# Layer scale on one core: pieces of 53, 11, 53, 11 rows with five loads, in place of 40, 37, 40, 11 with seven

## The chip, the cores and the metric

One of the eight cores of a Trainium2 chip. The metric is the device time of one execution in microseconds (us).

## The reference

```python
B, S, D = 1024, 16, 512          # bfloat16: x, y of [B, S, D], gamma of [D]
def reference(x, y, gamma):
    return x + gamma * y
```

That is 16,384 rows of 512 elements: 16.78 MB of x, as much of y, and as much to write.

## The kernel before

Each of the 128 partitions holds 128 rows of 1 KB. y has a buffer of its full size and the result is computed in it; x has one that is smaller than x, so a later load of x reuses the place of an earlier one. An entry of the list is one transfer: kind, first row, end row, and for x the place in its buffer.

```python
PIECES = [40, 37, 40, 11]       # VectorE's pieces
SP  = [('x', 0, 40, 0), ('y', 0, 40), ('x', 40, 77, 40), ('y', 40, 77),
       ('y', 77, 128), ('x', 77, 117, 0), ('x', 117, 128, 40)]      # queue of loads
ACT = [('g',), ('s', 0, 64), ('s', 64, 128)]                        # gamma, two stores
RELEASE = ('x', 77, 117, 0)     # its landing lets the first store go
DVE = [('m', 0), ('a', 0), ('m', 1), ('a', 1), ('m', 2), ('a', 2), ('m', 3), ('a', 3)]
# ... (cut)
            if need > known:                      # x: the adds that free its place
                eng.wait_ge(s_add, need)          # s: the adds that make its rows
# ... (cut)
        if kind == "m":                           # y = y * gamma
            need(y_loads, c)                      # wait for the loads of this piece
            nc.vector.tensor_tensor(out=yt, in0=yt, in1=g, op=MULT).then_inc(s_dve, 1)
            open_mults += 1
        else:                                     # y = x + y
            need(x_loads, c)
            if open_mults:                        # wait for the open multiplies
                _take(s_dve, open_mults, nc.vector)
                open_mults = 0
            at = x_at(starts[c])
            xt = x_sb[:, at : at + PIECES[c], :]
            nc.vector.tensor_tensor(out=yt, in0=xt, in1=yt, op=ADD).then_inc(s_add, 1)
```

gamma is spread over the partitions by a matmul with a row of ones and copied to SBUF. The first store waits for its adds and for the landing of the RELEASE load, so that it does not meet the loads in the DMA engines.

Of the kernel before, what the change touches and what calls it, by code (L numbers as in the profile page):

```python
# [3 lines left out]


PIECES = [40, 37, 40, 11]



SP = [('x', 0, 40, 0), ('y', 0, 40), ('x', 40, 77, 40), ('y', 40, 77), ('y', 77, 128), ('x', 77, 117, 0), ('x', 117, 128, 40)]  # L10
ACT = [('g',), ('s', 0, 64), ('s', 64, 128)]

EARLY = (2, 1)


RELEASE = ('x', 77, 117, 0)

DVE = [('m', 0), ('a', 0), ('m', 1), ('a', 1), ('m', 2), ('a', 2), ('m', 3), ('a', 3)]
MULT, ADD = mybir.AluOpType.mult, mybir.AluOpType.add


def _take(sem, n, eng):


    return eng.wait_ge(sem, n).then_inc(sem, -n)  # L25


def kernel(
# [18 lines left out]
    rows = N // P  # L47
    n = len(PIECES)
    assert sum(PIECES) == rows
    starts = [sum(PIECES[:c]) for c in range(n + 1)]  # L50
    dt = xf.dtype
# [7 lines left out]
    y_sb = nc.alloc_sbuf_tensor("y_sb", [P, rows, D], dt).ap()  # L59
    x_loads = [w for w in SP + ACT if w[0] == "x"]  # L60
    y_loads = [w for w in SP + ACT if w[0] == "y"]
    stores = [w for w in SP + ACT if w[0] == "s"]
    for loads in (x_loads, y_loads, stores):
# [8 lines left out]
    s_add, s_go, s_rel, s_end, s_out = sem("s_add"), sem("s_go"), sem("s_rel"), sem("s_end"), sem("s_out")  # L72
    added = [a for kind, *a in DVE if kind == "a"]
    order = {a[0]: k for k, a in enumerate(added)}

    def meets(a, b, c, d):
        return a < d and c < b

    def pieces_of(a, b):
        return [c for c in range(n) if meets(starts[c], starts[c + 1], a, b)]  # L80

    def x_at(row):
        return next(w[3] + row - w[1] for w in x_loads if w[1] <= row < w[2])

    def frees(w):

        old = x_loads[: x_loads.index(w)]
        old = [v for v in old if meets(v[3], v[3] + v[2] - v[1], w[3], w[3] + w[2] - w[1])]
        return [c for v in old for c in pieces_of(v[1], v[2])]

    early = []

    def ring(eng, what, n_early):

        known, went = 0, False
        for k, w in enumerate(what):
            kind = w[0]
            need = frees(w) if kind == "x" else pieces_of(w[1], w[2]) + list(w[3:]) if kind == "s" else []
            need = max((order[c] + 1 for c in need), default=0)
            if kind == "s" and not went:  # L100
                _take(s_go, 1, eng)
                went = True
            if need > known:
                eng.wait_ge(s_add, need)
                known = need
            if kind == "g":
                i = eng.dma_start(out=gamma_row, in_=gamma.unsqueeze(0)).then_inc(s_gamma, 16)
            elif kind == "x":
                to = x_sb[:, w[3] : w[3] + w[2] - w[1], :]
                i = eng.dma_start(out=to, in_=xv[:, w[1] : w[2], :]).then_inc(s_load[w], 16)  # L110
            elif kind == "y":
                r = slice(w[1], w[2])
                i = eng.dma_start(out=y_sb[:, r, :], in_=yv[:, r, :]).then_inc(s_load[w], 16)
            else:
                r = slice(w[1], w[2])
                i = eng.dma_start(out=ov[:, r, :], in_=y_sb[:, r, :]).then_inc(s_out, 16)
            if k < n_early:
                early.append(i.ins)

    ring(nc.sync, SP, EARLY[0])  # L120
    ring(nc.scalar, ACT, EARLY[1])
# [9 lines left out]

    _take(s_load[RELEASE], 16, nc.tensor)
    nc.tensor.sem_inc(s_go, 1)
# [4 lines left out]
    def need(loads, c):  # L138
        for w in loads:
            if w not in landed and meets(starts[c], starts[c + 1], w[1], w[2]):  # L140
                if w == RELEASE:
                    _take(s_rel, 1, nc.vector)
                else:
                    _take(s_load[w], 16, nc.vector)
                landed.add(w)

    for kind, *args in DVE:
        c = args[0]
        yt = y_sb[:, starts[c] : starts[c + 1], :]
        if kind == "m":  # L150
            need(y_loads, c)
            g = gamma_sb[:, None, :].to_broadcast([P, PIECES[c], D])
            nc.vector.tensor_tensor(out=yt, in0=yt, in1=g, op=MULT).then_inc(s_dve, 1)  # L153
            open_mults += 1
        else:
# [4 lines left out]
# [3 lines that stand above are left out]
# [44 lines left out]
```

## Time and profile before

| | before |
|---|---|
| time, median of 3 | 119.99 us (119.98 to 120.29) |
| span of the profiled run | 118.8 us |
| VectorE busy | 70.2 us, 59% |
| packets of both queues, share of 16 DMA engines | 98.6% |

The page gives busy time by engine and the share that the queues' packets take of all 16 DMA engines. The view by stretches gives, for each stretch of time, its length, the busy time of PE, PEld, DVE (VectorE) and POOL with the number of instructions, the granted clock, the mean DMA share and GB/s. A packet counts where it starts, so a short stretch can show a share over 1, and zero between two rounds of long packets that all engines are in. A hole is seen only when the next round's start comes later than the packet's length. The lines are in the prediction below.

### The profile page before, as it was taken

Reading aid. Unit: us, or ns where it says so; the run is one execution under the profiler, and the core shown is the slowest. Engines: PE = TensorE matmul, PEld = TensorE weight load, DVE = VectorE, ACT = ScalarE, POOL = GpSimd, SP = SyncE. Lnnn points to the kernel's source line nnn. Section 1 sums busy time; section 2 is a strip of 40 time slices with the busy share of each in tenths; the row PEclk is TensorE's granted clock in tenths of the full one; section 3 lists DMA queues with packets and bytes.
Section 4 is the critical chain, followed back from the end, with each engine's and each line's share of the span. In section 5 each row is a group of like instructions: output and inputs, shape, how many; then the busy total and the mean of one; then the engine's idle time right before and its main releaser. Section 6 shows DMA issues by size and latency. Waiting matters only on the chain. (4 is left out here: it accounts for less than half of the span.)

```text
span 118.8 us, 84 instructions
## 1 busy us (share of the span) xinstructions
PE 0.6 (0%) x1; PEld 0.1 (0%) x1; DVE 70.2 (59%) x10; POOL 0.2 (0%) x4
## 2 busy tenths in 40 slices
PE   0100000000000000000000000000000000000000
PEld 0000000000000000000000000000000000000000
DVE  0020000009999999799999999999999980000000
POOL 0000000000000000000000000000000000000000
DMA  7999999999999999989696999998899889988890
GB/s 221 442 441 441 441 441 441 441 425 408 408 421 472 485 459 408 475 369 563 281 563 262 441 414 441 408 637 353 353 530 530 353 353 397 662 353 353 353 684 22
DMA packets 1298, 50.33 MB, mean 424 GB/s; under 512 B 145, under 2 KB 146, under 8 KB 146
## 3 DMA queue, kind: packets, MB, share of 16 engines
q1 hardware_dynamic: 1008, 33.55, 66.0%
q10 hardware_dynamic: 290, 16.78, 32.6%
HBM read 33.56 MB, written 16.78 MB: 424 GB/s over the span
## 5 line engine op out<-in xcount | busy, mean ns | idle before, releaser
L153 DVE TENSOR_TENSOR y_sb<-y_sb,gamma_sb 128x20480 bf16<-128x20480 bf16 (+2 forms) x4 | 34.8, 8688 | 20.6 <-DVEq L25 20.6
L162 DVE TENSOR_TENSOR y_sb<-x_sb,y_sb 128x20480 bf16<-128x20480 bf16 (+2 forms) x4 | 34.8, 8691 | 0.6
L129 DVE CAST gamma_sb<-gamma_ps 128x512 bf16<-128x512 f32 x1 | 0.7, 690 | 4.1 <-DVEq L25 4.1
L124 DVE MEMSET ones_row<- 1x128 bf16 x1 | 0.2, 165 | 2.0 <-PEq L41 2.0
L127 PE MATMUL gamma_ps<-gamma_row,ones_row 1*128 1x512 bf16 x1 | 0.6, 581 | 5.5 <-PEq L25 5.5
L127 PEld LDWEIGHTS gamma_ps<-gamma_row,ones_row 1*128 1x128 bf16 x1 | 0.1, 98 | 5.5 <-issue 5.5
L191 POOL MEMSET const-bfloat16-1.0<- 128x1 bf16 x1 | 0.1, 102 | 0.0
L191 POOL MEMSET const-uint8-127<- 128x1 uint8 x1 | 0.1, 101 | 0.0
L191 POOL MEMSET const-float32-0.0<- 128x1 f32 x1 | 0.1, 99 | 0.2 <-issue 0.2
L191 POOL MEMSET const-float32-1.0<- 128x1 f32 x1 | 0.1, 98 | 0.0
## 6 DMA issues: line engine op xcount, KB each, us to landing
x_sb<-in_x_dram SPq DMA_DIRECT2D x2, 5120.0 KB, 21.3
y_sb<-in_y_dram SPq DMA_DIRECT2D x1, 6528.0 KB, 61.8
y_sb<-in_y_dram SPq DMA_DIRECT2D x1, 5120.0 KB, 26.3
x_sb<-in_x_dram SPq DMA_DIRECT2D x1, 4736.0 KB, 36.0
y_sb<-in_y_dram SPq DMA_DIRECT2D x1, 4736.0 KB, 46.9
x_sb<-in_x_dram SPq DMA_DIRECT2D x1, 1408.0 KB, 10.6
out_dram<-y_sb ACTq DMA_DIRECT2D x2, 21.8
gamma_row<-in_gamma_dram ACTq DMA_DIRECT2D x1, 1.0 KB
```

The source lines that it names most:

```text
L124: nc.vector.memset(ones_row, 1.0).then_inc(s_ones, 1)
L127: nc.tensor.matmul(gamma_ps, ones_row, gamma_row, start=True, stop=True).then_inc(s_ps, 1)
L129: nc.vector.tensor_copy(out=gamma_sb, in_=gamma_ps).then_inc(s_dve, 1)
L153: nc.vector.tensor_tensor(out=yt, in0=yt, in1=g, op=MULT).then_inc(s_dve, 1)
L162: nc.vector.tensor_tensor(out=yt, in0=xt, in1=yt, op=ADD).then_inc(s_add, 1)
L191: nc = _bacc.Bacc("TRN2", target_bir_lowering=False, num_devices=1)
```

## The change

Its intent is fewer, larger loads (five of 64, 64, 64, 53 and 11 KB a partition) that line up with the two 64-row stores, while the release of the first store stays with the last load but one.

```diff
-PIECES = [40, 37, 40, 11]
-SP = [('x', 0, 40, 0), ('y', 0, 40), ('x', 40, 77, 40), ('y', 40, 77), ('y', 77, 128), ('x', 77, 117, 0), ('x', 117, 128, 40)]
+PIECES = [53, 11, 53, 11]
+SP = [('y', 0, 64), ('x', 0, 64, 0), ('y', 64, 128), ('x', 64, 117, 0), ('x', 117, 128, 64)]
-RELEASE = ('x', 77, 117, 0)
+RELEASE = ('x', 64, 117, 0)
-DVE = [('m', 0), ('a', 0), ('m', 1), ('a', 1), ('m', 2), ('a', 2), ('m', 3), ('a', 3)]
+DVE = [('m', 0), ('m', 1), ('a', 0), ('a', 1), ('m', 2), ('m', 3), ('a', 2), ('a', 3)]
 # ... (cut: a load of x now waits only for the pieces whose rows it really
 #      overwrites, so the 53-row load waits for the first add alone)
```

I call the loads y0, x0, y1, x2, x3 in their order, and the adds first to last.

More of the change, by code (lines that the diff above doesn't have):

```diff
@@ L85, in frees @@
     def frees(w):
-        old = x_loads[: x_loads.index(w)]
-        old = [v for v in old if meets(v[3], v[3] + v[2] - v[1], w[3], w[3] + w[2] - w[1])]
-        return [c for v in old for c in pieces_of(v[1], v[2])]
+        c = set()
+        for v in x_loads[: x_loads.index(w)]:
+            lo, hi = max(v[3], w[3]), min(v[3] + v[2] - v[1], w[3] + w[2] - w[1])
+            if lo < hi:
+                c |= set(pieces_of(v[1] + lo - v[3], v[1] + hi - v[3]))
+        return sorted(c)
     early = []
```

## The prediction

> **What bounds the kernel now.** I read the page first: who is busy, and how many bytes move.
>
> ```profile
> span 118.8 us, 84 instructions
> ...
> PE 0.6 (0%) x1; PEld 0.1 (0%) x1; DVE 70.2 (59%) x10; POOL 0.2 (0%) x4
> ...
> q1 hardware_dynamic: 1008, 33.55, 66.0%
> q10 hardware_dynamic: 290, 16.78, 32.6%
> HBM read 33.56 MB, written 16.78 MB: 424 GB/s over the span
> ```
>
> VectorE works 59% of the span, but the packets of the two queues take 66.0 + 32.6 = 98.6% of what 16 DMA engines have. Every byte is needed once: x and y in, the result out. The chain of waits is no help here: it stops after one 3.09 us add, because what ends the span is a store that the chain does not count as work. So I cut the span into stretches and ask for the DMA share in each (last two columns: DMA share and GB/s). A packet is booked in the stretch where it starts, so I put the cuts in the pauses between rounds of packets.
>
> ```profile
> 0.00:1.00 1.00, 0.00 (x0) 0.00 (x0) 0.00 (x0) 0.20 (x4) 1.00 0.00 0
> 1.00:2.90 1.90, 0.00 (x0) 0.00 (x0) 0.17 (x1) 0.00 (x0) 1.00 1.15 345
> 2.90:48.00 45.10, 0.58 (x1) 0.10 (x1) 21.70 (x3) 0.00 (x0) 1.00 1.00 433
> 48.00:63.40 15.40, 0.00 (x0) 0.00 (x0) 14.59 (x3) 0.00 (x0) 1.00 1.01 434
> 63.40:75.60 12.20, 0.00 (x0) 0.00 (x0) 12.20 (x2) 0.00 (x0) 1.00 0.99 430
> 75.60:79.00 3.40, 0.00 (x0) 0.00 (x0) 3.40 (x1) 0.00 (x0) 1.00 0.93 394
> 79.00:98.30 19.30, 0.00 (x0) 0.00 (x0) 18.14 (x4) 0.00 (x0) 1.00 1.02 440
> 98.30:117.60 19.30, 0.00 (x0) 0.00 (x0) 0.00 (x0) 0.00 (x0) 1.00 1.00 435
> ```
>
> From 1.0 us to the end no stretch is idle. The 0.93 before 79.0 is made up by the 1.02 after it (two 11 KB packets' worth on the far side of the cut). Loads in pieces of 37 to 51 KB a partition and stores of 64 KB run at the same 433 GB/s. Above all there is no hole at 98.4, where the first store hands over to the second, nor at 79, where loads hand over to stores. The whole: 50.33 MB / 0.4334 MB per us = 116.1 us; the remaining 2.7 us of the span are the 1.0 us to the first packet, about 0.6 us by which the first packets are longer than later ones (next ones start at 3.0 to 3.7), and the spread of the 16 engines with the completion at the end. The only things worth asking of a change are therefore: does it take bytes away (no), does it shorten those 2.7 us (hardly), does it open a hole?
>
> The timeline gives the issues that could open one, and the groups by shape give VectorE's durations:
>
> ```profile
> 1.90 0.33 SPq L110 DMA_DIRECT2D x_sb<-in_x_dram  x1
> ...
> 2.28 0.95 SPq L113 DMA_DIRECT2D y_sb<-in_y_dram  x2
> ```
>
> ```profile
> 48.67 0.33 SPq L110 DMA_DIRECT2D x_sb<-in_x_dram  x1
> ```
>
> ```profile
> 94.35 3.09 DVE L162 TENSOR_TENSOR y_sb<-x_sb,y_sb 128x5632 bf16<-128x5632 bf16 x1
> 97.47 0.34 ACTq L116 DMA_DIRECT2D out_dram<-y_sb  x1
> ```
>
> ```profile
> L162 DVE TENSOR_TENSOR y_sb<-x_sb,y_sb 128x20480 bf16<-128x20480 bf16 x2 | 21.6, 10824 | 0.3
> ...
> L162 DVE TENSOR_TENSOR y_sb<-x_sb,y_sb 128x5632 bf16<-128x5632 bf16 x1 | 3.1, 3091 | 0.1
> ```
>
> The third x load reuses the first one's buffer; it is issued at 48.67, right after the add that frees it, while the queue has loads until 63.6. The last add ends at 97.44 and the second store is issued at 97.47; its first packets start at 98.4. So an issue needs under about 1 us to its first packet, as the very first load does (0.00 to 1.0), and the second store came only just in time.
>
> **What the Trainium skill says.** "DMA: Bandwidth & Descriptors", section "Where 436 GB/s comes from", gives a fabric ceiling of 435 GB/s for the 16 engines; the trace's 433 sits on it, so nothing is to be had from other piece sizes. The same page, "Issuing engines are not separate DMA queues", says that transfers issued by different engines share the same 16 DMA engines; the trace agrees: loads on one queue and stores on the other never add up to more than 433 over several rounds. Its "Queues, rings and completion order" says that an engine with work on several rows takes turns packet by packet; this matters for the 11-row load and the first store, below. "VectorE: DVE Perf Modes", section "The perf-mode tier table", caps a bf16 tensor_tensor at 2x, two elements a cycle at 0.96 GHz, 0.5208 ns an element; the trace has (10824 - 3091) / (20480 - 5632) = 0.5208 ns.
>
> **The change part by part.** One row of all 128 partitions is 131,072 bytes, 0.3024 us at 433.4 GB/s. I call the loads in order y0, x0, y1, x2, x3.
>
> Removed: two loads of the seven, and the early order x, y, x, y. Bytes, both stores, the number and total size of VectorE operations, and the release by the last load but one stay. The fewer joints between loads: from the second round (3.37 us) to the start of the 40-row load at 63.9, 200 rows took 60.6 us, and at the rate of the store rounds (2.42 us for 8 rows, 0.3022 a row) they would take 60.45. Larger loads can save 0.15 us at most.
>
> Arrivals, worked from arrivals of before. y0 (64 rows): the 80th row landed at 0.42 + 26.3 = 26.7; 16 rows less, 21.9. x0 (128 rows): the 117th landed at 1.90 + 36.0 = 37.9; 11 more, 41.2. y1 (192 rows): the 154th landed at 2.28 + 46.9 = 49.2; 38 more, 60.7.
>
> VectorE: 53 rows are 27,136 elements, 10.824 + 6,656 x 0.0005208 = 14.29 us; 11 rows 3.09. Total 4 x (14.29 + 3.09) = 69.5, as now 69.6. The two multiplies run from 22.0 to 36.3 and to 39.3; VectorE then waits 2 us for x0; the adds run 41.3 to 55.6 and to 58.7.
>
> The new tight spot: x2 now waits for the first add, so it is issued at about 55.7, not 48.7. The loads before it are used up when? The 51-row load's packets started at 48.2 after 154 rows; 38 rows later is 59.7. With 1 us from issue to packet, x2 is ready at 56.7: 3.0 us to spare. So the ring doesn't run dry, and x2 lands after 245 rows in all, exactly as now. The ACT queue's first store goes at about 77.0 as now (77.07), and x3, 11 rows, covers the way to it for 3.3 us as now. x3 needs no buffer wait (rows 64 to 75 are fresh).
>
> Second half: the multiplies run from 60.8 to 75.1 and to 78.1, the adds, after x2 landed at 76.9, from 78.3 to 92.5 and to 95.6. The second store is issued at 95.7, 1.8 us sooner than now, but its packets still cannot start before the first store's are done at 98.4. Gain on the path: zero; it only gets more slack.
>
> Sum: bytes 0, start 0, joints -0.1, hand-overs 0, end 0. Span 118.7; the measured time stands 1.2 us above the span (119.99 and 118.8), so 119.9.
>
> **Rivals.** First: x2 late. If x0 lands late, or its issue takes longer, the queue has a hole of g, and release, stores and end all move by g. To cost 2% it must be 2.4 us, so the first add would have to end near 61.1 rather than 55.6; the VectorE rows scatter by 3 ns and the landings follow from rates that hold within 1%. A hole of some tenths is conceivable: 120.2.
>
> Second: the first store takes turns with x3. Then each of x3's eight packets per engine would wait 2.42 us behind a store packet, x3 would land after 8 x 2.84 = 23 us at about 99, the last add would end near 102, and the second store would leave a hole of about 4 us: 124. The trace of before shows no turns taken with the same 11 rows and the same store (11 KB packets run without a break until the stores start at 79.1), and the change keeps that geometry. I give it 2%.
>
> Third: the earlier end of VectorE is worth its 1.8 us: 118.2, for which the second store would have to be late now. The stretch from 98.3 begins with packets at once, so I do not believe it; and even then it is under 2%.
>
> Fourth: y and x loads of 64 KB run at another rate. 1% of 33.55 MB is 0.8 us; stores of 64 KB and loads of 51 KB give no sign of it.
>
> **Range and chances.** The kernel's own runs spread over 0.3 us. With 0.15 to gain and some tenths to lose, 119.5 to 120.4 should hold it 8 times in 10. Faster by 2% would mean 117.6, under what bytes at 433 GB/s plus the unchanged start and end allow: 1%. Slower by 2% needs rival one or two in full: 3%. Within 2%: 96%.
>
> **What would show it right or wrong.** DMA share 0.99 to 1.01 in every stretch from 2.9 to 117.6, no hole near 60 and none near 98; x2 issued at 55.7 and the first store at 77.0; the second store issued at 95.7, not 97.5, with the end unmoved. A stretch without packets at 59 to 61, x3 landing after 90, or a load rate other than 433 would make it wrong.

## The result and the profile after

119.97 us median of 6 runs (119.88 to 120.17), against 119.99 of 6 (119.98 to 120.29). The ratio is 0.9994, 95% interval 0.9981 to 1.0007. Ratios here are the mean time of one kernel's fast runs over that of the other's of the same rounds, so not quite the ratio of the medians. The time is the same.

The page of the changed kernel, the lines that answer to those of before:

```profile
span 118.6 us, 78 instructions
...
PE 0.6 (0%) x1; PEld 0.1 (0%) x1; DVE 70.0 (59%) x10; POOL 0.2 (0%) x4
...
q1 hardware_dynamic: 720, 33.55, 66.0%
q10 hardware_dynamic: 290, 16.78, 32.6%
```

The queue of loads has 720 packets instead of 1008 and takes the same 66.0%. The stretches, cut again in the pauses between rounds:

```profile
2.90:40.00 37.10, 0.58 (x1) 0.10 (x1) 17.98 (x3) 0.00 (x0) 1.00 0.98 424
40.00:59.00 19.00, 0.00 (x0) 0.00 (x0) 17.29 (x2) 0.00 (x0) 1.00 1.02 442
59.00:75.00 16.00, 0.00 (x0) 0.00 (x0) 14.38 (x2) 0.00 (x0) 1.00 1.01 434
...
79.00:98.30 19.30, 0.00 (x0) 0.00 (x0) 16.36 (x2) 0.00 (x0) 1.00 1.01 437
98.30:117.60 19.30, 0.00 (x0) 0.00 (x0) 0.00 (x0) 0.00 (x0) 1.00 1.00 435
```

No hole: 0.98 and 1.02 are the two sides of a cut through a round. The timeline has the issues, and the groups by shape the long add:

```profile
55.70 0.81 SPq L113 DMA_DIRECT2D x_sb<-in_x_dram  x2
...
76.89 18.83 ACTq L119 DMA_DIRECT2D out_dram<-y_sb  x2
```

```profile
95.39 0.34 ACTq L119 DMA_DIRECT2D out_dram<-y_sb  x1
```

```profile
L165 DVE TENSOR_TENSOR y_sb<-x_sb,y_sb 128x27136 bf16<-128x27136 bf16 x2 | 28.6, 14292 | 2.3 <-DVEq L25 2.2
```

x2 was issued at 55.70 (worked out: 55.7), the first store at 76.89 (77.0), the second at 95.39 (95.7), and the 53-row add took 14.292 us (14.29). The second store is issued 2.1 us sooner than before (97.47), and the span ends 0.2 us sooner.

One thing was not in the prediction. The matmul that spreads gamma waits for a load of 1 KB, and started later, before (first fence) and after:

```profile
5.49 0.58 PE L127 MATMUL gamma_ps<-gamma_row,ones_row 1*128 1x512 bf16 x1 [5.49 <-PEq L25]
```

```profile
7.10 0.58 PE L130 MATMUL gamma_ps<-gamma_row,ones_row 1*128 1x512 bf16 x1 [7.10 <-PEq L25]
```

It costs nothing, as y0 lands at 21.9. I come back to it, since it shows how queues share an engine.

### The profile page after: what moved, and what is told of

Its sections match the earlier page's. It is cut to its first block, busy times and chain, and to the rows that moved or that the text cites. A ratio compares the mean times of both kernels' runs of the same rounds, so it can differ in the third digit from the quotient of the medians.

```text
span 118.6 us, 78 instructions
## 1 busy us (share of the span) xinstructions
PE 0.6 (0%) x1; PEld 0.1 (0%) x1; DVE 70.0 (59%) x10; POOL 0.2 (0%) x4
## 5 line engine op out<-in xcount | busy, mean ns | idle before, releaser
L156 DVE TENSOR_TENSOR y_sb<-y_sb,gamma_sb 128x27136 bf16<-128x27136 bf16 (+1 forms) x4 | 34.6, 8688 | 15.4 <-DVEq L25 15.4
L165 DVE TENSOR_TENSOR y_sb<-x_sb,y_sb 128x27136 bf16<-128x27136 bf16 (+1 forms) x4 | 34.6, 8689 | 2.3 <-DVEq L25 2.2
## 6 DMA issues: line engine op xcount, KB each, us to landing
x_sb<-in_x_dram SPq DMA_DIRECT2D x1, 6784.0 KB, 20.8
```

## The experiments

The theory: the bytes at 433 GB/s set the time; an earlier VectorE, fewer joints and another order are worth nothing while no DMA engine runs dry; the change has some slack at each place where a transfer waits for VectorE. The main rivals: VectorE's path sets the end, or a gain was eaten by a loss. The kernel before, run beside each batch, had medians of 119.96 to 119.98 us. Idle work below means a multiply on VectorE whose result goes to a free part of the x buffer and is not used. All outputs were correct but the one that is wrong. Most losses below are under 2% of the time; what tells them from noise is an interval that leaves out 1. A few readings below are of single packets: they come from the start, length and size of each packet in the packed traces, as the views give only sums.

**Bytes alone: a shorter second store** (wrong)

```diff
-ACT = [('g',), ('s', 0, 64), ('s', 64, 128)]
+ACT = [('g',), ('s', 0, 64), ('s', 64, 117)]
```

> The changed kernel with a second store of 53 rows instead of 64: wrong on purpose (the last 11 rows of each partition are not written). Theory (bytes at 433 GB/s): 11 x 0.3024 = 3.3 us less, 116.6 to 116.7. Rival (a latency or VectorE sets the end): 120.0, or less than half of that gain.

116.57 us in one run (state unknown). 3.4 us less for 1.44 MB less, within 0.1 us of the rate. Bytes set the end.

**VectorE's order of before**

```diff
-DVE = [('m', 0), ('m', 1), ('a', 0), ('a', 1), ('m', 2), ('m', 3), ('a', 2), ('a', 3)]
+DVE = [('m', 0), ('a', 0), ('m', 1), ('a', 1), ('m', 2), ('a', 2), ('m', 3), ('a', 3)]
```

> The changed kernel with VectorE's order of before (multiply, add, multiply, add). Theory: the first add still ends at 55.6 (it waits for x0, not for VectorE), so x2 and the release are unmoved; the last add ends near 97.4 instead of 95.3, as in the kernel before, and the second store comes just in time: 120.0, plus 0.2 at most. Rival (VectorE's earlier end is a gain that pays for a loss elsewhere in the change): up to 1.8 us slower, 121.8.

120.07 us, ratio 1.0005 (0.9988 to 1.0021). The second store was issued at 98.06, 2.7 us later than with the changed order (I had expected 97.4; the third add had to wait for x2 until 77.5), and the time hardly moved. So no gain from VectorE's earlier end pays for a loss.

**Where the earlier end went: the same idle work in both kernels, ahead of the third add**

```diff
+            if c == 2:                        # in the kernel before: place 51 for 53
+                nc.vector.wait_ge(s_add, 2)   # long met; for the order of accesses
+                nc.vector.tensor_tensor(out=x_sb[:, 53:64, :], in0=y_sb[:, 0:11, :], in1=g, op=MULT).then_inc(s_dve, 1)
+                _take(s_dve, 1, nc.vector)
             at = x_at(starts[c])
```

> The changed kernel with one idle-work multiply of 11 rows (3.1 us and a wait) ahead of the third add, so that the last add and the second store come about 3.2 us later. Theory: second store issued at 98.6 instead of 95.4, packets from 99.6, where the engines are free from 98.5 to 98.9; the end moves by 0.7 to 1.1 only: 120.7 to 121.1. Rival (the end of VectorE sets the end of the kernel): 123.2.

> The kernel before with the same idle-work multiply ahead of its third add. Theory: here the second store was issued at 97.5, just in time, so it is issued at 100.7, packets from 101.7, engines free from 98.4 to 99.1: the end moves by 2.6 to 3.2, to 122.6 to 123.2; about 2 us more than the changed kernel loses by the same work. Rival (both kernels have the same slack at the end): the same loss in both.

Changed kernel 120.77 us (ratio 1.0068, 1.0053 to 1.0083), kernel before 122.70 (1.0227, 1.0210 to 1.0244): plus 0.8 and plus 2.7. The stretches around the start of the second store, the changed kernel with the idle work first, then the kernel before with it:

```profile
98.00:99.40 1.40, 0.00 (x0) 0.00 (x0) 0.62 (x1) 0.00 (x0) 1.00 0.01 0
99.40:99.70 0.30, 0.00 (x0) 0.00 (x0) 0.00 (x0) 0.00 (x0) 1.00 8.19 3495
```

```profile
98.00:101.50 3.50, 0.00 (x0) 0.00 (x0) 2.64 (x1) 0.00 (x0) 1.00 0.00 0
101.50:101.70 0.20, 0.00 (x0) 0.00 (x0) 0.00 (x0) 0.00 (x0) 1.00 12.27 5243
```

The first store's last packets end near 98.5 in both. The second store's start at 99.5 where it was issued at 98.65, and at 101.5 where it was issued at 100.67: 0.8 to 0.9 us from issue to packets in a queue that has run dry. The theory's numbers hold for both: the 2.1 us by which the change ends VectorE sooner became slack of the second store.

**Release by the last load**

```diff
-RELEASE = ('x', 64, 117, 0)
+RELEASE = ('x', 117, 128, 64)
```

> The changed kernel with the first store released by the last load (x3) instead of the last but one. Theory (a DMA engine has a hole wherever the next transfer is issued less than about 1 us before it is needed): x3 lands at about 79.95, store issued at 80.0, packets from 81.0, engines free from 79.1 to 79.6: hole of 1.5 to 1.9 us, 121.5 to 121.9. Rival (the release does not matter, the store's wait for its adds was met at 58.7): 120.0.

121.98 us, ratio 1.0172 (1.0157 to 1.0187). The store was issued at 80.69 rather than the 80.0 that I had worked out, its packets started at 81.6, and no packet of data starts before that from 79.6 on:

```profile
79.60:81.50 1.90, 0.00 (x0) 0.00 (x0) 1.90 (x1) 0.00 (x0) 1.00 0.00 0
```

This hole in the DMA engines is paid in full: 2.0 us are lost. So the release by the last load but one matters: x3 covers the way to the store.

**Release by the second y load: load and store meet**

```diff
-RELEASE = ('x', 64, 117, 0)
+RELEASE = ('y', 64, 128)
```

> The changed kernel with the first store released by the second y load (landing about 60.6), so that it meets x2 in the engines. If an engine takes turns between the two queues packet by packet: x2's eight packets an engine wait for a 2.42 us store packet each, x2 lands near 95.5, third add to 109.8, last add to 112.9, second store's packets from 113.9 where the engines are free at about 98.5: a hole of about 15 us, 135. If an engine finishes a load's packets before it turns to the store: nothing changes, 120.0. If only bytes count and order is free: 120.0.

131.70 us in one run (state unknown). The stretches:

```profile
66.00:90.00 24.00, 0.00 (x0) 0.00 (x0) 12.44 (x2) 0.00 (x0) 1.00 1.02 443
...
92.40:100.20 7.80, 0.00 (x0) 0.00 (x0) 7.80 (x1) 0.00 (x0) 1.00 0.75 319
100.20:110.40 10.20, 0.00 (x0) 0.00 (x0) 9.34 (x2) 0.00 (x0) 1.00 0.00 0
```

While both queues have work the engines are full (1.02), but x2 takes 36.4 us from issue to landing instead of 20.8, the third add waits for it until 92.25, and the DMA engines have no data from 99.8 to 110.4. So an engine does take turns, and with the release left out of the plan the same bytes cost 11.7 us. My 135 was too high: x2 landed at 92.0, not 95.5, since the store was issued at 60.97 and its first packets started only at 66.7, after each engine had run two more packets of x2.

**Smaller loads: joints** (a joint is where one load follows another in the queue)

```diff
-SP = [('y', 0, 64), ('x', 0, 64, 0), ('y', 64, 128), ...
+SP = [('y', r, r + 16) for r in range(0, 64, 16)] + [('x', r, r + 16, r) for r in range(0, 64, 16)] + [('y', r, r + 16) for r in range(64, 128, 16)] + [...
```

> The changed kernel with its first three loads cut into twelve of 16 rows: 14 loads in all instead of 5, packets of 16 KB instead of 64 KB. Theory (a joint between loads costs 0.03 us at most, and the size of packets doesn't matter to the rate): 9 more joints, 120.0 to 120.3. Rival (each load has a cost of its own, so that two loads fewer were a gain which something else in the change ate): with 0.3 us or more for each, 122.5 and up.

120.53 us of 6 runs, ratio 1.0047 (1.0033 to 1.0060). The 9 further joints, with packets of a quarter of the size, cost 0.56 us, 0.06 each: twice the bound that I had set and far below the rival. The first store is issued at 77.62 instead of 76.89, so the loads are where it is lost. The lengths of the packets tell what costs it. The median 16 KB packet took 0.612 us, and a quarter of a 64 KB packet is 0.6045 (2.418 / 4); over the 96 such packets of an engine that is 0.72 us, as much as the store is late. So it is the number of packets that costs, and no cost of a joint beside it is seen. The medians of all sizes lie on one line: 0.309 us for 8 KB, 0.422 for 11, 0.612 for 16, 1.213 for 32, 1.514 for 40, 2.004 for 53 and 2.418 for 64, which is 0.010 us for each packet and 0.0376 us for each KB (about 435 GB/s over 16 engines), within 0.002 us. The change has two loads and so 16 packets fewer on each engine: by this line 0.16 us, a gain that the interval of the result (0.23 us faster to 0.08 slower) allows but cannot show.

**The disputed slack: delay of the first add.** Idle work of 3, 7 and twice 11 rows ahead of the first add, so that x2, which waits for it, is issued later.

```diff
+            if c == 0:                          # late1: (3,)  late2: (7,)  late6: (11, 11)
+                for r in (7,):
+                    nc.vector.tensor_tensor(out=x_sb[:, 64:64 + r, :], in0=y_sb[:, 0:r, :], in1=g, op=MULT).then_inc(s_dve, 1)
+                    _take(s_dve, 1, nc.vector)
             at = x_at(starts[c])
```

> The changed kernel with an idle-work multiply of 7 rows (about 2.0 us and 0.15 us of waiting) on VectorE just ahead of the first add. Theory (the DMA engines set the time, and the reuse of the x buffer has about 3 us to spare): the first add ends at about 57.8 instead of 55.6, x2 is issued at 57.9, its packets could start at 58.9, the ring is fed until 59.6; so no hole, and the time stays at 120.0 within 0.2. Rival (the change has used up the slack, VectorE's path through the first add sets the end): the time grows by the 2.2 us, to 122.2.

> The same with two idle-work multiplies of 11 rows (twice 3.09 us and waits, about 6.4 us) ahead of the first add. Theory: x2 is issued at 62.1, its packets start at 63.1 where the ring ran dry at 59.6 to 60.1; a hole of 3.0 to 3.5 us at 60, and all that follows, the end too, moves by that: 123.0 to 123.5. Rival (no slack): plus 6.4, 126.4. Rival (loads are hidden anyway): 120.0.

> The run with 2.2 us of idle work ahead of the first add lost 2 to 3 us although x2 was issued at 58.0, 1.6 us before the ring ran dry; so the spare 3 us of the prediction were wrong. Here the idle work has 3 rows (1.0 us and a wait, about 1.1 us): x2 issued at 56.8. Theory A (an engine's next load must be in its queue when it starts the last packet that it has, 57.2 to 57.6, and an issue needs about 1 us to get there): 57.8 is too late, the engines start x2 unevenly, and the time is 121 to 123. Theory B (what counts is the lead of the issue over the end of the last packets, and 2.8 us are enough): 120.0 within 0.2.

| delay | x2 issued at | time, us | more than 119.97 |
|---|---|---|---|
| none (the change) | 55.70 | 119.97 | |
| 3 rows | 56.81 | 120.86, ratio 1.0074 (1.0035 to 1.0114) | 0.9 |
| 7 rows | 58.01 | 122.50, ratio 1.0214 (1.0172 to 1.0256) | 2.5 |
| 11 and 11 rows | 62.16 | 124.17, one run, state unknown | 4.2 |

The theory's 3 us of slack fell. The rival (no slack, VectorE's path sets the end) comes near with 7 rows, 122.2 against 122.50, but falls with 22 rows, where it forecast 126.4. The last packets of y1 start at about 57.2 to 57.7 in all four and last 2.4 us, so x2's should start from 59.6. The stretches in which x2's first 16 packets start, for the change, the 3-row, the 7-row and the 22-row delay:

```profile
59.50:60.30 0.80, 0.00 (x0) 0.00 (x0) 0.00 (x0) 0.00 (x0) 1.00 2.52 1086
60.30:61.20 0.90, 0.00 (x0) 0.00 (x0) 0.58 (x1) 0.00 (x0) 1.00 0.00 0
```

```profile
59.50:60.30 0.80, 0.00 (x0) 0.00 (x0) 0.29 (x1) 0.00 (x0) 1.00 2.41 950
60.30:61.20 0.90, 0.00 (x0) 0.00 (x0) 0.57 (x1) 0.00 (x0) 1.00 0.29 121
```

```profile
59.50:60.30 0.80, 0.00 (x0) 0.00 (x0) 0.80 (x1) 0.00 (x0) 1.00 1.98 746
60.30:61.20 0.90, 0.00 (x0) 0.00 (x0) 0.90 (x2) 0.00 (x0) 1.00 0.55 181
61.20:61.70 0.50, 0.00 (x0) 0.00 (x0) 0.50 (x1) 0.00 (x0) 1.00 0.41 109
```

```profile
59.50:63.00 3.50, 0.00 (x0) 0.00 (x0) 3.50 (x2) 0.00 (x0) 1.00 0.00 0
63.00:63.70 0.70, 0.00 (x0) 0.00 (x0) 0.70 (x1) 0.00 (x0) 1.00 3.85 1241
```

A packet of x2 is 53 KB, 54.3 thousand bytes. GB/s times the length of a stretch, over that, counts them: the change starts all 16 by 60.3 (1086 x 0.80 / 54.3). With the 7-row delay 11 start by then, 3 by 61.2 and 1 more by 61.7; the sixteenth comes later still, and 11 of the 16 took 2.3 to 3.3 us instead of 2.0. The delay stays to the end of x2, whose landing is that of its last packet: that packet started at 77.4 there, against 74.1 in the change, the first store was issued at 80.10 instead of 76.89, and the span grew by those 3.2 us in the profiled execution. With the 3-row delay 14 start by 60.3 and 2 by 61.2, and the loss is 0.9. With the 22-row delay the queue is dry and restarts evenly, 1.0 us after the issue; its cost is the hole of 3.4 us and first packets of about 2.7 us instead of 2.0 (together more than the 3.0 to 3.5 forecast).

So a load that was issued this late behind running loads started unevenly. Theory B of the 3-row delay falls. Theory A (it must be there when an engine starts its last packet) has only the direction right: all last packets had started by 57.7, before its 57.8, yet 14 engines of 16 went on without a wait, and 120.86 lies under its 121 to 123.

A store shows no such loss. In the kernel before, the second store was issued at 97.47, only 1.0 us before the first engine came free, while each engine was in its last packet of the first store; all 16 of its first packets start from 98.47 to 99.06, and the engines waited 0.2 us in all, summed over the 16:

```profile
98.40:99.10 0.70, 0.00 (x0) 0.00 (x0) 0.00 (x0) 0.00 (x0) 1.00 3.48 1498
```

After an empty queue, too, the first packets of a load are longer (about 2.7 us instead of 2.0 with the 22-row delay), those of a store hardly (2.46 instead of 2.42 in the idle-work runs). Why the two differ is not shown.

To part the theories by another knob, the second y load was cut, so that the last packets before x2 are short, with the 7-row delay left in:

```diff
-('y', 64, 128)
+('y', 64, 120), ('y', 120, 128)
```

> The run with 2.2 us of idle work ahead of the first add, with the second y load cut into 56 and 8 rows, so that the last packets before x2 are of 8 KB (0.3 us) and start at 59.3 to 59.8 instead of 57.2 to 57.6; x2 is issued at 58.0 as there. Theory A: 59.0 is ahead of the start of the last packets, x2 follows without a hole and evenly, and the loss is gone: 120.0 to 120.3. Theory B (the lead in us counts, and 1.6 is too little): the loss stays, 122 to 123.

Inconclusive. The four executions took 122.39, 122.16, 119.88 and 120.05 us. The first two are over 1.5% above the fastest and so classed as slow (the clock was 1.000 in all); over the fast two the ratio is 0.9998 (0.9976 to 1.0019). Without the cut four of four lost 2 us or more. The profiled execution is one of the long ones, and in it x2's packets start unevenly again. A lead of 1.6 us can thus be enough, against theory B, but the cut puts the issue at the edge and not clear of it. What exactly an engine needs, and by when, stays open.

**An attempt to beat both: two queues for the first load**

```diff
-SP = [('y', 0, 64), ...     ACT = [('g',), ...                EARLY = (2, 1)
+SP = [('y', 0, 32), ...     ACT = [('g',), ('y', 32, 64), ...  EARLY = (2, 2)
```

> An attempt at the 2.7 us which are not bytes: the first y load is split, 32 rows on the SP queue and 32 rows on the ACT queue behind gamma, so that an engine has a second queue to turn to while the first packets of the first one come. If the longer first packets (0.6 us) are a latency that another queue can hide: 119.4 to 119.8. If they are paid once by each engine whatever is queued: 120.0.

122.42 us of 6 runs, ratio 1.0186 (1.0156 to 1.0217): neither of the two expectations. The timeline shows why:

```profile
26.63 17.30 DVE L156 TENSOR_TENSOR y_sb<-y_sb,gamma_sb 128x27136 bf16<-128x27136 bf16 x2 [20.53 <-DVEq L25]
44.07 17.29 DVE L165 TENSOR_TENSOR y_sb<-x_sb,y_sb 128x27136 bf16<-128x27136 bf16 x2
58.39 0.80 SPq L113 DMA_DIRECT2D x_sb<-in_x_dram  x2
```

The SP queue went on to x0 while the ACT queue still had y rows; they took turns, y was complete at 26.6 instead of 21.9, the first add ended at 58.4, and x2 was issued at 58.39, where the delay experiment has a loss of about 2.5 us. Here VectorE did no idle work and x2's first packets still started unevenly, from 59.9 to 61.4, so the loss does not need the idle work. The start itself did not get shorter either: first packets of 32 KB start at 1.0 and the next ones at 2.9 to 3.1, while a later round of them takes 1.2 us. No version beat the two kernels.

## Why the prediction was right or wrong, point by point

- **The bound.** Right and shown: 11 rows less to store took 3.4 us off, and the holes that the runs opened in the DMA engines were paid. "Nothing is to be had from other piece sizes" holds here to 0.2 us: each packet costs 0.010 us beside its bytes.
- **Arrivals and VectorE's durations.** Right: x2's issue within 0.1 us, the release within 0.2, the second store within 0.3.
- **The earlier end of VectorE is worth nothing on the path.** Right: 2.7 us later or 2.1 us earlier, the same time. It is slack, shown by the unequal loss of 0.8 and 2.7 us under equal idle work.
- **Joints, at most 0.15 us.** Right in size (0.16 us by the packets' lengths), but what costs is each packet and not the joint; the 0.03 us a joint of the theory for smaller loads was too low.
- **"3.0 us to spare" for x2.** Wrong. The step that failed is "With 1 us from issue to packet, x2 is ready at 56.7". I took the 1 us from the first load, which found the engines empty, and from a store behind a store. For a load behind running loads, 1.1 us of delay already cost 0.9 us, and 2.3 us cost 2.5. The spare time was under 1.1 us. The change falls on the right side of that; as far as this step goes, the prediction held by luck.
- **Rival one, "the first add would have to end near 61.1" to cost 2%.** Wrong with it: an end at 58.0 cost 2.1% (1.7 to 2.6).
- **Rival two, turns between store and load.** Rightly judged not to happen, but not for want of turns: released at y1, the store does take turns and 11.7 us are lost. With the release kept, each engine ended its x3 packets before its first packet of the store, though the store was issued at 76.89 and each engine began three more packets of x3 after 77.9, where the store could have started by the 0.8 to 1.0 us measured above. What kept them apart was that the store's first turn came late.
- **Small slips, without consequence.** Nine 11 KB packets, not two, start after the cut at 79.0. The 1.2 us between time and span compares a median with a profiled execution that took 120.14 us; for one execution it is 1.3. The 0.96 GHz and the elements a cycle that stand beside the tier table are in the sections "Specifications" and "Terms" of "VectorE: DVE Perf Modes", and the 0.5208 ns given with them is an estimate worked out from these, which the trace bears out.

## What to carry to other kernels

When bytes set the time, an engine that ends sooner, or fewer and larger transfers, buy slack and not time; ask of a change only whether a DMA engine runs dry, and measure the slack of a waiting transfer by adding known idle work, in both kernels. A load that waits for its buffer has to be issued well before the queue ahead of it is in its last packets: here the change cut the lead from 15 us (63.6 - 48.7) to 3.9 (59.6 - 55.7) without a loss, and at 2.8 there was one, while a store behind a store needed no more than 1.0. Large packets in one queue also delayed the one small transfer that shared the engines, gamma.

## What the Trainium skill lacked or had wrong

- "DMA: Bandwidth & Descriptors", section "Where 436 GB/s comes from", which the prediction cites for its 435, also says that between HBM and SBUF the HBM side, about 358 GB/s, is what binds. Here, with a program on one core, 433 GB/s were read and written, so it did not bind (the 425 measured that the section itself quotes is above it too).
- The same page, section "Latency and other measured facts", gives about 0.6 us to the first byte for transfers issued from SP or ACT, and does not say from when it counts. Here a dry queue had its first packets 0.8 to 1.0 us after the issue began (98.65 to 99.5, 100.67 to 101.5, 62.16 to 63.1), which is 0.5 to 0.6 after the issuing instruction of 0.33 us ended; so no error of the page is shown. What the section lacks is the case behind a running queue: a load issued at 58.01, with its engines free from about 59.6, had its sixteen first packets start from 59.8 to 61.9.
- The same page, "Queues, rings and completion order", says that an engine takes turns packet by packet and that a packet typically has 9 to 17 descriptors. Turns are seen: gamma's 1 KB started at 2.29, 2.95, 3.46 and 4.17 us beside packets of 16, 32, 40 and 64 KB, after the first packet of its engine, and its completion after the next one, so that its matmul started at 3.41, 4.68, 5.49 and 7.10. But what the profile counts as a packet is one partition's part of a load, of any size here (720 of five loads: 128 each, and 16 for the completion). What the section lacks is how late a queue gets its first turn beside one that is running: the store that was released early waited for two more packets of x2 (53 KB), the first store of the changed kernel for three more of x3 (11 KB). Why is not shown.
- No page gives the cost of a joint between loads. Here there is none to be seen beyond 0.010 us for each packet.
